# Another order of the first loads, eight zero products and fewer copies of the means at the start of a fused attention and two-layer MoE kernel

## The chip, the cores and the metric

The kernel runs on one core of a Trainium2 chip. The metric is the device time of one launch in microseconds. Three timed runs of the kernel before took 476.56, 477.20 and 478.63 us; the median is 477.2 us. The trace is of one further execution, taken with the hardware profiler.

## The reference

Everything is float32. For 2 batches, 8 heads, 768 positions and head size 64, each query attends to the keys less than 16 positions away and to 24 block summaries (for keys the maximum over 32 positions, for values the mean). The result, 1536 tokens of 512 values, goes through two feed-forward layers.

```python
k_sum = k.reshape(B, H, nb, block, D).max(axis=3)
v_sum = v.reshape(B, H, nb, block, D).mean(axis=3)
scores_l = scale * np.matmul(q, k.transpose(0, 1, 3, 2))          # kept where |i - j| < 16
scores_s = scale * np.einsum('bhsd,bhnd->bhsn', q, k_sum) + np.log(block)
a = softmax(np.concatenate([np.where(mask_l, scores_l, -1e9), scores_s], axis=-1))
x = np.matmul(a, np.concatenate([v, v_sum], axis=2))              # to [1536, 512]
h = x @ w_in                                                      # 512 -> 1024
ln = layernorm(h * softmax(h)) * g_ln
x = ln @ w_out                                                    # 1024 -> 512
h = x @ w_in2; g = elu(h); out = g @ w_out2                       # 512 -> 2048 -> 512
```

## The kernel before

A *unit* is 64 queries of one batch, all 8 heads: 24 units, 12 for each batch. For a unit the kernel makes scores (`attn_s`: a window of 96 keys and the 24 summaries, 120 columns for a pair of heads), the softmax, the transposes of the probabilities (`attn_p`) and, for two units together, the product with v (`attn_x`), whose result `x_ps` is written as a high and a low part (`xT`) for the first feed-forward layer. There (`ffn1_in`) every product is three products of high and low parts (L108 to L110), and so are those behind it. The words of w_in come as 64-bit numbers; each of the 8 blocks of 512 KB goes through a conversion on four engines: L126 on ScalarE, L129 on GpSimd, L130 and L134 on VectorE, then the high part on ScalarE (L138) and the low part on VectorE (L105).

The means of a batch's values (`sum_v`) are products of all its v rows with a small matrix `avg`: six blocks of 256 KB for batch 1 (b = 0), three of 512 KB for batch 2 (b = 1), whose rows VectorE first adds in pairs (L196). The names are the kernel's, which counts batches from 0: the text calls them batch 1 and batch 2. For b = 0 the 24 rows of means go from PSUM to `vsum` (L199, ScalarE), and `attn_x` copies them on GpSimd (L101) into the rows 96 to 119 of the four v buffers `vws`, whose rows 0 to 95 are loaded for each unit (`load_v`).

The order has two sources. On SyncE, which issues all loads, it is the order of the code (a manual schedule): `load_k(0)`, `load_q(1)`, `load_v(0)` and so on in the listing below. On the other engines a scheduler sets it when the program is built, from the order of the code as a priority and its own model of the engines; each engine then works through its list in order. So a moved load or a new instruction can change the lists of all engines. The lists before and after are in the same order again for the last 1753 of some 2340 instructions on TensorE and the last 190 of 213 on SyncE.

At the start, 32 products of zeros (L478) run on TensorE while the first transfers are on their way. Scores, transposes, products with v, means and the other small results share one pool of four PSUM buffers (tag `b`).

Of the kernel before, what the change touches and what calls it, by code (L numbers as in the profile page):

```python
# [24 lines left out]
WIN = 96  # L25
# [13 lines left out]
NV = 4  # L39
# [14 lines left out]
def tile_kernel(ctx: ExitStack, tc: tile.TileContext, qd, kT, v, w_in, w_out, g_ln, w_in2, w_out2,  # L54
# [113 lines left out]
    def load_k(b):  # L168
        k_sb[b] = p_k.tile([128, NP, S + 2 * PAD], F32, tag="k", name="k_sb", bufs=2)
        for p in range(NP):  # L170
            nc.sync.dma_start(k_sb[b][:, p, :], kT[b, p])
# [9 lines left out]
    def sum_v(b):  # L181
        pst = psb.tile([128, DM], F32, tag="b", name="vs_ps")
        v_sb = p_k.tile([128, NP, S + 2 * PAD], F32, tag="k", name="v_sb", bufs=2).rearrange("p a s -> p (a s)")
        m = 2 if b else 1
        n = S // (128 * m)
        if b:
            pairs_d = avg_d.rearrange("(r two) c -> r two c", two=2)[:, 0, :]
            nc.sync.dma_start(avg[0:64, 8:], pairs_d[:, 8:])
            nc.sync.dma_start(avg[64:128, 8:], pairs_d[:, 4:124 + NB])
        for i in range(n):  # L190
            vt = v_sb[:, i * m * DM:(i + 1) * m * DM].rearrange("p (s d) -> p s d", s=m)
            r0 = PAD + i * 128 * m
            nc.sync.dma_start(vt, v[b, r0:r0 + 128 * m, :].rearrange("(p s) d -> p s d", s=m))
            c0 = NB - i * 4 * m
            if b:
                nc.vector.tensor_tensor(vt[:, 0], vt[:, 0], vt[:, 1], op=ALU.add)  # L196
            nc.tensor.matmul(pst, lhsT=avg[:, c0:c0 + 128], rhs=vt[:, 0], start=i == 0, stop=i == n - 1)
        vsum[b] = p_at.tile([128, DM], F32, tag="vsum", name="vsum", bufs=1)
        nc.scalar.activation(vsum[b][WIN:KW, :], pst[WIN:KW, :], AF.Copy)  # L199

    def load_q(n):
        q_bd[n] = p_at.tile([128, NP, 2 * TQ], F32, tag="q", name="q_bd", bufs=4)
        nc.sync.dma_start(q_bd[n], qd[n])
# [13 lines left out]
    def attn_s(n):  # L217
        b, t = divmod(n, NT)
        j, half = divmod(n, 2)
        kw = kws[n % NKW]  # L220
        if n not in q_bd:
            load_q(n)
        if t < NKW and n:
            copy_pool(kw[:, :, WIN:KW], ksum[b])
        if n < NCOPY:
            copy_pool(kw[:, :, 0:WIN], k_sb[b][:, :, t * TQ:t * TQ + WIN])
        sps = psb.tile([128, NP, 128], F32, tag="b", name="s_ps")
        for p in range(NP):
            nc.tensor.matmul(sps[:, p, 0:KW], lhsT=q_bd[n][:, p, :], rhs=kw[:, p, :], start=True, stop=True)  # L229
        sm = p_at.tile([128, NP, KW], F32, tag="sm", name="sm", bufs=NBUF)  # L230
        st = p_at.tile([128, 4, NP], F32, tag="st", name="st", bufs=NBUF)
        nm, ss, ri = (st[:, i, :] for i in range(3))
        mi = 1 if t == 0 else (2 if t == NT - 1 else 0)
        for p in range(NP):
            nc.vector.tensor_tensor_reduce(sm[:, p, :], sps[:, p, 0:KW], mask[:, mi, :], -scale, 3.0e38,  # L235
                                           op0=ALU.add, op1=ALU.min, accum_out=nm[:, p:p + 1])
        for p in range(NP):
            nc.scalar.activation(sm[:, p, :], sm[:, p, :], AF.Exp, bias=nm[:, p:p + 1], scale=-1.0,  # L238
                                 accum_out=ss[:, p:p + 1])
        nc.vector.tensor_scalar(ri, ss, 1e-9, None, op0=ALU.add)  # L240
        nc.vector.reciprocal(ri, ri)  # L241
        for p in range(NP):
            nc.gpsimd.tensor_scalar(sm[:, p, :], sm[:, p, :], ri[:, p:p + 1], 1.0, op0=ALU.mult, op1=ALU.mult)  # L243
        live[n] = sm
    def attn_p(n):
        pps = psb.tile([128, NP, 128], F32, tag="b", name="p_ps")
        for p in range(NP):
            nc.tensor.transpose(pps[:KW, p, :], live[n][:, p, :], ident)  # L248
        pT = p_at.tile([128, NP, 128], F32, tag="pT", name="pT")
        nc.scalar.activation(pT[:KW], pps[:KW], AF.Copy)  # L250
        live[n] = pT

    def attn_x(j):
        xT[j] = [p_at.tile([128, NP, 128], F32R, tag=f"x{i}", name="xT", bufs=3) for i in range(2)]
        xps = psb.tile([128, NP, 128], F32, tag="b", name="x_ps")
        for half in (1, 0):
            n = 2 * j + half
            b, t = divmod(n, NT)
            if b == 0 and t < NV:
                copy_pool(vws[n % NV][WIN:KW, :], vsum[b][WIN:KW, :])  # L260
        todo_x = [(half, p, hh) for half in (1, 0) for p in range(NP) for hh in range(2)]

# [191 lines left out]
    def more(n=1):  # L454
        for _ in range(n):
            if conv:
                conv.pop(0)()
# [16 lines left out]
    zero = ln_t[:, 4, 0:256].bitcast(BF16)  # L474
    nc.vector.memset(ln_t[:, 4, 0:256], 0.0)
    busy = psh.tile([128, F1], F32, tag="h", name="busy")
    for i in range(32):
        nc.tensor.matmul(busy[:, 0:512], lhsT=zero[:, 0:128], rhs=zero, start=True, stop=True)  # L478

    loads = tc.manual_schedule(engines={mybir.EngineType.SP})  # L480
    loads.__enter__()
    load_k(0)
    load_q(1)
    load_v(0)
    nc.sync.dma_start(mask, mask_d)
    sum_k(0)
    nc.sync.dma_start(ident, ident_d)
    load_q(0)
    more()
    nc.sync.dma_start(avg, avg_d)  # L490
    attn_s(0)
    more()
    attn_s(1)
    sum_v(0)
    more(2)
    attn_p(0)
    attn_p(1)
    attn_s(2)
    load_v(1)
    attn_x(0)  # L500
    nc.sync.dma_start(gT, g_ln)
    attn_s(3)
# [301 lines left out]
```

## Time and profile before

| | us |
|---|---|
| median of three runs | 477.2 (476.56 to 478.63) |
| the profiled execution | 476.27 |
| its span in the trace | 474.5 |
| TensorE products busy (PE) | 460.4, 97% of the span |
| weight loads (PEld, beside the products) | 388.4, 82% |
| VectorE (DVE) | 300.1, 63% |
| ScalarE (ACT) | 288.2, 61% |
| GpSimd (POOL) | 116.9, 25% |
| DMA, 82.74 MB | mean 174 GB/s over the span |

A busy share is a mean over the whole span. The stretches differ: the first 37 us move 350 GB/s, those from 100 to 400 us 145 GB/s. In the rows, a time is counted from the span's start; "idle before <- X" is the time for which the engine had nothing running before an instruction and what ended that time; L numbers are lines of the listing. The granted clock of TensorE is 1.00 in all stretches up to 400 us.

### The profile page before, as it was taken

The page shows a single profiled execution, that of the slowest core. Times are in us where ns is not written, and L with a number is a line of the kernel's source. Part 1 is how long each engine was busy: PE and PEld are TensorE (multiplying, and loading weights), DVE is VectorE, ACT ScalarE, POOL GpSimd, SP SyncE. Part 2 cuts the span into 40 slices and gives each one's busy share as a digit, 9 for nine tenths or more (in the row PEclk, how much of TensorE's full clock was granted, in tenths as well). Part 3 has the DMA queues.
Part 4 walks back from the last instruction along what each step waited for, and adds up shares of the span by engine and source line. Part 5 has one row for each costly group of instructions (what it writes and reads, how often), then busy time and mean ns, then how long its engine had stood idle before and what let it go on. Part 6 is the DMA issues. An engine that isn't in the chain of part 4 may idle for free.

```text
span 474.5 us, 7422 instructions
## 1 busy us (share of the span) xinstructions
PE 460.4 (97%) x2597; PEld 388.4 (82%) x2597; DVE 300.1 (63%) x668; ACT 288.2 (61%) x647; POOL 116.9 (25%) x209
## 2 busy tenths in 40 slices
PE   7779999999999999999999999999999999999996
PEld 3556888899989999999888888888888888888884
DVE  3789889875477448986989972476657555460001
ACT  1796899976576537667766762487667665560001
POOL 2786585762444113422132000000000000000000
PEclk9999999999999999999999999999999999999998
DMA  8998987812352424597798324532121221488012
GB/s 272 357 355 296 340 253 228 251 48 84 115 166 83 128 90 133 174 370 255 230 368 329 138 89 135 175 133 90 44 90 44 88 90 45 138 330 259 27 44 89
DMA packets 39989, 82.74 MB, mean 174 GB/s; under 512 B 9648, under 2 KB 18608, under 8 KB 39952
## 3 DMA queue, kind: packets, MB, share of 16 engines
q1 hardware_dynamic: 39808, 82.14, 51.7%
q8 instruction: 20, 0.33, 0.3%
q14 instruction: 17, 0.14, 0.1%
q10 hardware_dynamic: 144, 0.13, 0.1%
HBM read 70.53 MB, written 11.53 MB: 173 GB/s over the span
## 4 chain that ended last, share of the span: by engine, by line
PE 87%; DMA 8%; DVE 2%; ACT 1%; issue 1%; SPq 0%; DVEq 0%; ACTq 0%
PE o_ps L110 9%; PE o_ps L109 9%; PE o_ps L108 9%; PE h L108 7%; PE h L109 7%; PE h L110 7%; PE c L110 5%; PE c L109 5%; PE c L108 5%; DMA y<-in_w_in 5%; PE y_ps L108 4%; PE y_ps L110 4%; PE y_ps L109 4%; PE s_ps L229 3%; PE x_ps L265 2%; PE p_ps L248 2%
## 5 line engine op out<-in xcount | busy, mean ns | idle before, releaser
L129 POOL TENSOR_SCALAR conv<-conv 128x512 f32<-128x512 f32 x48 | 33.8, 705 | 81.2 <-ACT conv L126 79.9
L108 PE MATMUL o_ps<-w4r,g_hl 128*128 128x512 f32 x128 | 49.8, 389 | 0.0
L243 POOL TENSOR_SCALAR sm<-sm,st 128x120 f32<-128x120 f32 x96 | 43.3, 469 | 26.6 <-DVE st L241 7.7
L109 PE MATMUL o_ps<-w4r,g_hl 128*128 128x512 f32 x128 | 49.8, 389 | 0.0
L110 PE MATMUL o_ps<-w4r,g_hl 128*128 128x512 f32 x128 | 45.4, 389 | 0.0
L108 PE MATMUL y_ps<-lnT,w_out 128*128 128x384 f32 x128 | 43.5, 340 | 0.2 <-ACT y L327 0.2
L109 PE MATMUL y_ps<-lnT,w_out 128*128 128x384 f32 x128 | 43.1, 337 | 0.0
L110 PE MATMUL y_ps<-lnT,w_out 128*128 128x384 f32 x128 | 42.8, 336 | 0.0
L108 PE MATMUL h<-w_in,xT 128*128 128x512 f32 x96 | 39.7, 415 | 1.9 <-ACT w_in L138 1.0
L110 PE MATMUL h<-w_in,xT 128*128 128x512 f32 x96 | 38.5, 401 | 0.3 <-DVE xT L105 0.3
L238 ACT ACTIVATE sm<-sm,st 128x120 f32<-128x120 f32 x96 | 36.7, 387 | 3.4 <-DVE st L235 2.5
L109 PE MATMUL h<-w_in,xT 128*128 128x512 f32 x96 | 38.5, 401 | 0.0
L605 ACT ACTIVATE y<-y 128x512 f32<-128x512 f32 x48 | 30.1, 629 | 0.8
L624 DVE COPY y<-o_ps 128x512 f32<-128x512 f32 x5 | 3.5, 691 | 42.9 <-PE o_ps L110 42.9
L235 DVE CUSTOM_DVE_ANT_0 sm<-s_ps,mask 128x120 f32<-128x120 f32 x96 | 21.7, 276 | 12.0 <-PE s_ps L229 11.9
L126 ACT ACTIVATE conv<-y 128x512 f32<-128x512 f32 x30 | 20.1, 675 | 14.2 <-DMA y<-in_w_in 11.7
L105 DVE TENSOR_TENSOR g_hl<-y,g_hl 128x512 fp32r<-128x512 f32 x32 | 22.0, 688 | 10.6 <-ACT g_hl L138 10.6
L229 PEld LDWEIGHTS s_ps<-kw,q_bd 128*128 128x128 f32 x192 | 24.1, 191 | 5.6 <-POOL kw L101 2.4
L130 DVE TENSOR_SCALAR conv<-conv 128x512 int32<-128x512 int32 x48 | 23.7, 493 | 7.5 <-POOL conv L129 7.5
L229 PE MATMUL s_ps<-kw,q_bd 128*128 128x120 f32 x192 | 25.3, 276 | 3.1 <-DMA q_bd<-in_qd 2.8
L109 PEld LDWEIGHTS o_ps<-w4r,g_hl 128*128 128x128 f32 x128 | 24.1, 188 | 5.0
L108 PEld LDWEIGHTS o_ps<-w4r,g_hl 128*128 128x128 f32 x128 | 24.0, 188 | 5.0
(155 smaller groups left out, 1217.2 us busy)
## 6 DMA issues: line engine op xcount, KB each, us to landing
w4r<-w4d SPq DMA_DIRECT2D x38, 512.0 KB, 3.3
y<-in_w_in SPq DMA_DIRECT2D x16, 512.0 KB, 6.2
w4d<-w3f SPq DMA_DIRECT2D x16, 512.0 KB, 3.2
y<-in_w_out SPq DMA_DIRECT2D x14, 512.0 KB, 5.3
q_bd<-in_qd SPq DMA_DIRECT2D x24, 256.0 KB, 5.2
bits<-in_w_out SPq DMA_DIRECT2D x10, 512.0 KB, 5.7
w4l<-w4d SPq DMA_DIRECT2D x10, 512.0 KB, 7.0
vw<-in_v SPq DMA_DIRECT2D x24, 192.0 KB, 5.7
```

Of the source, the lines that this page charges most:

```text
L105: nc.vector.tensor_tensor(out_, x, hi.bitcast(F32), op=ALU.subtract)
L108: nc.tensor.matmul(ps, lhsT=l[0][ls], rhs=r[0][rs], start=first, stop=False, skip_group_check=parts)
L109: nc.tensor.matmul(ps, lhsT=l[0][ls], rhs=r[1][rs], start=False, stop=False, skip_group_check=parts)
L110: nc.tensor.matmul(ps, lhsT=l[1][ls], rhs=r[0][rs], start=False, stop=last, skip_group_check=parts)
L126: first = nc.scalar.activation(x, high.bitcast(F32), AF.Prelu, scale=TO_F32, alpha=SIGN_TO_28)
L129: nc.gpsimd.tensor_scalar(x, x, MOST, LEAST, op0=ALU.min, op1=ALU.max)
L130: nc.vector.tensor_scalar(a, a, 3, None, op0=ALU.logical_shift_left)
L229: nc.tensor.matmul(sps[:, p, 0:KW], lhsT=q_bd[n][:, p, :], rhs=kw[:, p, :], start=True, stop=True)
L235: nc.vector.tensor_tensor_reduce(sm[:, p, :], sps[:, p, 0:KW], mask[:, mi, :], -scale, 3.0e38, op0=ALU.add, op1=ALU.min, accum_out=nm[:, p ...
L238: nc.scalar.activation(sm[:, p, :], sm[:, p, :], AF.Exp, bias=nm[:, p:p + 1], scale=-1.0, accum_out=ss[:, p:p + 1])
L243: nc.gpsimd.tensor_scalar(sm[:, p, :], sm[:, p, :], ri[:, p:p + 1], 1.0, op0=ALU.mult, op1=ALU.mult)
L605: nc.scalar.activation(m, m, AF.Exp, scale=-1.0)
```

## The change

Five edits, all at the start of the program.

- `sum_v(0)` has no `vsum` tile of its own: ScalarE writes the means into `vws[0]`, and VectorE writes them from PSUM into `vws[1]`. `attn_x` copies only for units 2 and 3, from `vws[0]`.
- Unit 0's queries are loaded right behind the keys, then the mask, then unit 1's queries; unit 0's v rows come behind the identity matrix.
- Unit 1's v rows are loaded behind the v rows of the means, ahead of blocks 2 and 3 of w_in ("words 2 and 3").
- Eight more products of zeros are ordered behind unit 1's scores, with high priority.
- `attn_s` returns its last product, so that these can be put behind it.

```diff
-        vsum[b] = p_at.tile([128, DM], F32, tag="vsum", name="vsum", bufs=1)
+        vsum[b] = p_at.tile([128, DM], F32, tag="vsum", name="vsum", bufs=1) if b else vws[0]
         nc.scalar.activation(vsum[b][WIN:KW, :], pst[WIN:KW, :], AF.Copy)
+        if b == 0:
+            nc.vector.tensor_copy(vws[1][WIN:KW, :], pst[WIN:KW, :])
...
-            nc.tensor.matmul(sps[:, p, 0:KW], lhsT=q_bd[n][:, p, :], rhs=kw[:, p, :], start=True, stop=True)
+            last = nc.tensor.matmul(sps[:, p, 0:KW], lhsT=q_bd[n][:, p, :], rhs=kw[:, p, :], start=True, stop=True)
...
+        return last
...
-            if b == 0 and t < NV:
+            if b == 0 and 1 < t < NV:
                 copy_pool(vws[n % NV][WIN:KW, :], vsum[b][WIN:KW, :])
...
-    for i in range(32):
-        nc.tensor.matmul(busy[:, 0:512], lhsT=zero[:, 0:128], rhs=zero, start=True, stop=True)
+    def keep_busy(n, after=None):
+        with tc.issue_after(after.ins) if after else ExitStack():
+            with tc.high_priority():
+                for i in range(n):
+                    nc.tensor.matmul(busy[:, 0:512], lhsT=zero[:, 0:128], rhs=zero, start=True, stop=True)
+
+    keep_busy(32)
...
     load_k(0)
+    load_q(0)
+    nc.sync.dma_start(mask, mask_d)
     load_q(1)
-    load_v(0)
-    nc.sync.dma_start(mask, mask_d)
     sum_k(0)
     nc.sync.dma_start(ident, ident_d)
-    load_q(0)
+    load_v(0)
     more()
     nc.sync.dma_start(avg, avg_d)
     attn_s(0)
     more()
-    attn_s(1)
+    keep_busy(8, attn_s(1))
     sum_v(0)
+    load_v(1)
     more(2)
     attn_p(0)
     attn_p(1)
     attn_s(2)
-    load_v(1)
     attn_x(0)
```

The loads on SyncE's list behind the keys, before (`q_bd` are queries, `vw` the v rows of a unit, `y` the words of w_in in their staging buffers, `v_sb` the v rows of the means):

```order
L203 DMA q_bd<-in_qd 128x512
L207 DMA vw_121<-in_v 96x512
L485 DMA mask<-in_mask 128x360
L487 DMA ident<-in_ident 128x128
L203 DMA q_bd<-in_qd 128x512
L117 DMA y_65<-in_w_in 128x1024
L490 DMA avg<-in_avg 128x152
L117 DMA y_65<-in_w_in 128x1024
L193 DMA v_sb<-in_v 128x512 x6
L117 DMA y_66<-in_w_in 128x1024 x2
L203 DMA q_bd<-in_qd 128x512
L207 DMA vw_122<-in_v 96x512
```

And in the changed kernel, the same stretch:

```order
L205 DMA q_bd<-in_qd 128x512
L494 DMA mask<-in_mask 128x360
L205 DMA q_bd<-in_qd 128x512
L497 DMA ident<-in_ident 128x128
L209 DMA vw_121<-in_v 96x512
L117 DMA y_65<-in_w_in 128x1024
L500 DMA avg<-in_avg 128x152
L117 DMA y_65<-in_w_in 128x1024
L193 DMA v_sb<-in_v 128x512 x6
L209 DMA vw_122<-in_v 96x512
L117 DMA y_66<-in_w_in 128x1024 x2
L205 DMA q_bd<-in_qd 128x512
```

The first queries are now those of unit 0, the second those of unit 1, and `vw_122` (unit 1's v rows) has passed two blocks of words and one of queries. Ahead of the first block of words stand the same five transfers.

VectorE's list around the three adds of batch 2 (`v_sb<-v_sb`), before (L130 and L134 are conversions of words, the first L105 writes the low part of a block of w_in, L240 and L241 belong to the softmax of units 5 and 4):

```order
L240 TENSOR_SCALAR st<-st 128x4
L196 TENSOR_TENSOR v_sb<-v_sb 128x512
L241 RECIPROCAL st<-st 128x4
L105 TENSOR_TENSOR w_in_90<-conv,w_in_89 128x512
L130 TENSOR_SCALAR conv<-conv 128x512
L196 TENSOR_TENSOR v_sb<-v_sb 128x512
L134 SCALAR_TENSOR_TENSOR conv<-y_67,conv 128x512
L240 TENSOR_SCALAR st<-st 128x4
L196 TENSOR_TENSOR v_sb<-v_sb 128x512
L241 RECIPROCAL st<-st 128x4
```

And now (two lines further down in the listing for L240 and L241):

```order
L196 TENSOR_TENSOR v_sb<-v_sb 128x512
L242 TENSOR_SCALAR st<-st 128x4
L130 TENSOR_SCALAR conv<-conv 128x512
L243 RECIPROCAL st<-st 128x4
L134 SCALAR_TENSOR_TENSOR conv<-y_67,conv 128x512
L196 TENSOR_TENSOR v_sb<-v_sb 128x512 x2
L242 TENSOR_SCALAR st<-st 128x4
L130 TENSOR_SCALAR conv<-conv 128x512
```

The low part of the block of w_in stands ahead of the first add now, the other four between the first and the second, and nothing between the second and the third.

TensorE's list around the means of batch 2 (`vs_ps`) up to the products of units 2 and 3 with v (`x_ps`), before:

```order
L248 MATMUL p_ps<-ident,sm 120x128 x3
L108 MATMUL h<-w_in_89,xT 128x512
L197 MATMUL vs_ps<-v_sb,avg 128x512
L109 MATMUL h<-w_in_90,xT 128x512
L110 MATMUL h<-w_in_89,xT 128x512
L197 MATMUL vs_ps<-v_sb,avg 128x512 x2
L108 MATMUL h<-w_in_89,xT 128x512
L229 MATMUL s_ps<-kw_119,q_bd 128x120 x4
L265 MATMUL x_ps<-pT,vw_124 64x64 x8
```

And now:

```order
L252 MATMUL p_ps<-ident,sm 120x128 x3
L109 MATMUL h<-w_in_90,xT 128x512
L110 MATMUL h<-w_in_89,xT 128x512
L197 MATMUL vs_ps<-v_sb,avg 128x512 x2
L108 MATMUL h<-w_in_89,xT 128x512
L197 MATMUL vs_ps<-v_sb,avg 128x512
L231 MATMUL s_ps<-kw_119,q_bd 128x120 x4
L269 MATMUL x_ps<-pT,vw_124 64x64 x8
```

The products of h that stood between the first mean and the second stand ahead of the first, and one stands ahead of the third mean instead of behind it. The eight zero products stand between unit 1's scores and the first mean of batch 1, where nothing stood.

## Rows read from the trace of the kernel before

**Rows 1.** Stretches A:B in us, busy time of each engine, granted clock, DMA share, GB/s.

```profile
2.50:37.00 34.50, 27.01 (x155) 16.47 (x153) 23.81 (x81) 20.28 (x67) 22.93 (x42) 1.00 1.03 350
...
55.00:100.00 45.00, 44.76 (x370) 38.76 (x369) 39.82 (x136) 44.19 (x134) 29.79 (x57) 1.00 0.78 235
```

**Rows 2.** What TensorE waited for, 40 to 460 us: total, times, longest.

```profile
PE s_ps L229 <- DVE xT L105: 0.2, 1, 0.2
PE y_ps L108 <- ACT y L327: 0.2, 1, 0.2
```

**Rows 3.** The chain of waits, 0 to 45 us: start, duration, what.

```profile
26.71 6.91 DMA v_sb<-in_v
...
38.54 1.12 PE vs_ps L197 x2
...
39.90 0.88 PE s_ps L229 x8
40.78 1.08 PE x_ps L265 x32
```

**Rows 4.** TensorE in order of time, 1 to 27 us: start, duration, idle before.

```profile
11.68 2.02 PE L229 MATMUL s_ps<-kw,q_bd 128*128 128x120 f32 x16 [1.90 <-DMA q_bd<-in_qd]
15.16 1.96 PE L197 MATMUL vs_ps<-v_sb,avg 128*128 128x512 f32 x4 [1.47 <-DMA v_sb<-in_v]
...
18.25 2.74 PE L197 MATMUL vs_ps<-v_sb,avg 128*128 128x512 f32 x6
...
22.36 1.12 PE L229 MATMUL s_ps<-kw,q_bd 128*128 128x120 f32 x8 [0.93 <-DMA q_bd<-in_qd]
...
26.82 0.50 PE L108 MATMUL h<-w_in,xT 128*128 128x512 f32 x1 [0.92 <-ACT xT L138]
```

**Rows 5.** ScalarE in order of time, 12 to 28 us.

```profile
12.87 0.69 ACT L126 ACTIVATE conv<-y 128x512 f32<-128x512 f32 x1 [10.87 <-DMA y<-in_w_in]
13.47 0.38 ACT L238 ACTIVATE sm<-sm,st 128x120 f32<-128x120 f32 x1
```

**Rows 6.** TensorE's weight loads in order of time, 0 to 14 us.

```profile
4.13 0.15 PEld L478 LDWEIGHTS <-ln 128*128 128x128 bf16 x1 [0.27 <-issue]
4.44 4.85 PEld L478 LDWEIGHTS <-ln 128*128 128x128 bf16 x23 [0.15 <-issue]
...
11.65 1.86 PEld L229 LDWEIGHTS s_ps<-kw,q_bd 128*128 128x128 f32 x16 [2.36 <-POOL kw L101]
```

**Rows 7.** GpSimd in order of time, 8 to 60 us: the means.

```profile
21.78 3.12 POOL L101 TENSOR_SCALAR vw<-vsum 24x512 f32<-24x512 f32 x4 [0.37 <-ACT vsum L199]
```

**Rows 8.** DMA issues from 27.9 to 28.1 us: count, KB, us to landing.

```profile
v_sb<-in_v SPq DMA_DIRECT2D x1, 512.0 KB, 7.9
```

**Rows 9.** A stretch, columns as in rows 1.

```profile
35.90:37.20 1.30, 1.20 (x5) 0.40 (x3) 1.30 (x4) 0.86 (x3) 1.30 (x2) 1.00 1.04 399
```

**Rows 10.** VectorE in order of time, 34.3 to 38.5 us.

```profile
34.74 0.69 DVE L196 TENSOR_TENSOR v_sb<-v_sb 128x512 f32<-128x512 f32 x1 [0.23 <-issue]
35.35 0.17 DVE L241 RECIPROCAL st<-st 128x4 f32<-128x4 f32 x1
35.44 0.66 DVE L105 TENSOR_TENSOR w_in<-conv,w_in 128x512 fp32r<-128x512 f32 x1
36.02 0.42 DVE L130 TENSOR_SCALAR conv<-conv 128x512 int32<-128x512 int32 x1
36.35 0.77 DVE L196 TENSOR_TENSOR v_sb<-v_sb 128x512 f32<-128x512 f32 x1
37.05 0.68 DVE L134 SCALAR_TENSOR_TENSOR conv<-y,conv 128x512 int32<-128x512 int32 x1
37.65 0.25 DVE L240 TENSOR_SCALAR st<-st 128x4 f32<-128x4 f32 x1
37.80 0.68 DVE L196 TENSOR_TENSOR v_sb<-v_sb 128x512 f32<-128x512 f32 x1
```

**Rows 11.** Groups of instructions, 9 to 100 us: count, busy, mean ns.

```profile
L294 DVE SCALAR_TENSOR_TENSOR ln<-h,ln 128x1024 f32<-128x1024 f32 x6 | 7.2, 1207 | 0.7 <-ACT ln L292 0.7
```

## The prediction

> **What bounds the kernel now.** I read the stretches first, then TensorE's waits. Between 2.5 and 37 us TensorE is busy for 27.0 of 34.5 us, and in the same stretch the DMA engines are busy all the time (share 1.03, 350 GB/s) [rows 1]. From 40 to 460 us TensorE waits only twice, for 0.2 us each [rows 2]. So the kernel has two halves. After 40 us the end is set by the sum of TensorE's work, of which the change moves only the order. Before 40 us the transfers set the pace, and what counts is when TensorE's queue gets past its last wait.
>
> The chain of waits says which that is: the transfer of batch 2's v rows (`v_sb<-in_v`), the third product of the means of batch 2 (38.54 us), the scores of unit 6 (39.90), the products with v of units 2 and 3 (40.78), and from there on TensorE alone [rows 3]. The reader should therefore ask of each edit one thing: does it bring forward the moment at which the products of units 2 and 3 start (40.78 us), and does it move work of TensorE from behind that moment to ahead of it? The second can be counted in the order: ahead of these products stand 16 products of h, 8 transposes and 4 groups of scores behind the first product of unit 1 with v, before as now. So only the first is left.
>
> **The change part by part.**
> Queries. Before, unit 0's queries are the ninth transfer and TensorE idles 1.90 us for them, from the end of the zero products to 11.68 us [rows 4]. Now they take the place of unit 1's, and the scores of unit 0 can start when the zero products end, at 9.8 us: 1.9 us earlier. What is queued behind them eats this. ScalarE's queue still has the first conversion of w_in ahead of all exponentials. That instruction waited 10.87 us for its words and started at 12.87, and the exponentials ran back to back from 13.47 on [rows 5]. The bytes ahead of those words are the same as before (queries, mask, identity, one v block, in another order), so they land at the same time, and the exponentials start at 13.47 again. Gain on the path: 0. If the words came with the scores, the whole 1.9 us would be there; that end I keep for a rival.
>
> Eight zero products behind unit 1's scores. At full rate the 23 loads for zero products of the start are (4.85 - 0.15) / 22 = 0.21 us apart, earlier ones 0.15 + 0.27 = 0.42 us apart [rows 6]. Eight are 1.7 to 3.4 us. They begin at about 11.5 to 12 us, and what follows, the means of batch 1, waits for v rows until 15.16 [rows 4], which have the same bytes ahead of them as before. Even at the slow rate they end at about 15.3. Cost 0; if that cover were gone it would be 1.7 us.
> Do they buy anything? The scores at 11.65, behind the longest idle stretch (1.90 us), load their weights 1.86 / 16 = 0.116 us apart [rows 6]; the scores of unit 6 at 39.90, with TensorE busy around them, take 0.88 us for eight, 0.110 each [rows 3]. Half the rate would show as twice the spacing. So the clock was not lost before. [...] By the row they only replace idle time that has done no harm.
>
> v rows of unit 1 ahead of words 2 and 3. One block of 192 KB moves ahead of 1,024 KB of words and 256 KB of queries; these come 0.5 to 0.7 us later (192 KB at 350 GB/s is 0.56). The scores of unit 2 waited 0.93 us for those queries and started at 22.36 [rows 4]; they stand ahead of the products of units 0 and 1 in TensorE's order and will start at about 23.0. Means to v buffers: the four copies on GpSimd took 3.12 us from 21.78 [rows 7]; now ScalarE writes one buffer directly, VectorE copies the second (0.6 to 0.7 us, by the other passes over 512 columns), and two copies are left. So both halves of x run together behind the scores of unit 2: 23.0 + 1.0 + 1.1 = 25.1 us, and h can start at 25.1 + 0.7 for xT's high half on ScalarE (its other passes over 512 columns take 0.69 [rows 5]) = 25.8 instead of 26.82 [rows 4]. That is 1.0 us, real and early. It isn't kept: the same 16 products of h then stand before the means of batch 2, which wait for v rows, so TensorE idles 1 us longer there.
>
> Those v rows. All bytes ahead of them are the same and the queue is never empty [rows 1], so they land as before. The second of three pieces, issued at 28.0, took 7.9 us and landed at 35.9 [rows 8]; the third is 512 KB more, at 399 GB/s 1.3 us [rows 9]: 37.2. VectorE adds each pair of rows. Before, the third add started at 37.80, with no idle time ahead of it [rows 10], so it came 0.5 us after its data: VectorE's order held it up. In the new order the low half of a converted word (L105) is gone from between the first add and the second, and the third add follows the second at once. By the starts of before [rows 10]: first add 34.74 + 0.61, then 0.15 (L240), 0.33 (L130), 0.09 (L241), 0.60 (L134): second add at 36.5, third at about 37.3, when its rows are there. On TensorE a means' product starts 0.74 us after its add (37.80 to 38.54), so the second at 37.26; its two passes take 0.86 (six take 2.74 with the last one's end [rows 4], 0.43 each), to 38.12; one product of h 0.23; the third means' product 38.35 to 39.21, and then the scores of unit 6. By the same count they started at 38.54 + 0.86 + 0.23 = 39.63 before. Difference 0.4 us. The ends: if VectorE gets to its adds no sooner, 0; if the third product follows the landing with nothing in between, 37.2 + 0.74 + 0.86 = 38.8 for the scores, 0.8 us.
>
> Sum: queries 0, zero products 0, v rows and means 0 (1.0 us gained and lost again), order of the adds -0.4, stalls behind 40 us as before. The profiled execution took 476.27 us for a span of 474.5; it becomes 475.9. The runs shown have their median at 477.2, 0.9 above it, so the forecast as a median is 476.8, with 476.4 to 477.2 as its own range.
>
> **The rivals.**
> The whole gain of the start arrives. If the scores' 1.9 us passed through, or the 1.9 and the 0.9 us at 26.82 together, the median would be 475.3 to 474.4. For it: TensorE's idle time before 37 us is 7.5 us, far more than that. Against it: DMA share 1.03 over the same stretch, and the same bytes ahead of the v rows of batch 2. It would need v rows that land earlier.
>
> Nothing changes. Between the first add and the second now stand an L240 that waits for unit 5's exponentials on ScalarE and an L130 that waits for GpSimd; if one of them is late by 0.4 us, so are the adds, and the gain is gone: 477.2.
>
> Slower, one mechanism: the passes over 1024 columns. Between 55 and 100 us ScalarE is busy for 44.2 of 45 us and VectorE for 39.8 [rows 1], and the one wait there is scores that need the buffer which xT's low half on VectorE gives back (0.2 us) [rows 2]. The instructions of this stretch stand in another order now, and in ScalarE's the exponential of the first h stands ahead of the third xT, where before it came after it. One pass of LayerNorm over 1024 columns on VectorE takes 1.21 us [rows 11]; wherever it now gets ahead of a low half of xT with less than that to spare, TensorE stalls for about 1 us. One such place against the 0.4 us gained gives 477.8, three give 479.8; from the first on the time is above the one before, from the third on by more than can be mistaken. Against it: before, an order of the same kind, with both engines as full, gave one stall of 0.2 us in 45 us.
>
> [...]
>
> **How the numbers follow.** Forecast 0.50 (476.8); whole gain 0.15; nothing 0.18; slower 0.15; clock 0.02. The range for 8 in 10 is 475.0 to 478.6: it leaves out the far part of the whole gain and the slower case from the second stall on. A time that differs by less than 0.5%, 2.4 us, can't be told from no change here. Faster by more than that: 0.06 of the whole gain (its far end, with luck in the stalls) and the clock's 0.02, 0.08. Slower by more than that: the slower case with three such places or more, 0.07. Within: 0.85.
>
> **What would show it right or wrong.** Scores of unit 0 at 9.8 to 10 us and the first exponential still at 13.4 to 13.5: the first step holds; an exponential before 12.9 breaks it. Zero products that end before 15.0 and a first product of the means at 15.0 to 15.3. Scores of unit 2 at 23.0, later than before, and h from about 25.8. A wait of TensorE of 1 us or more for the first add of batch 2, then the third add at 37.2 to 37.4, and products of units 2 and 3 at 40.1 to 40.6. From there to 460 us idle time of TensorE under 1 us in all. I am wrong if the products of units 2 and 3 start before 39.9, since then the transfers did not hold them, or if TensorE stalls by more than 1.5 us behind 40 us.

## The result: slower, 479.8 us against 476.6, and the profile after

The changed kernel has a median of 479.76 us (22 runs, 477.85 to 482.13), the kernel before, run beside it, 476.63 us (22 runs). The ratio is 1.0059, with an interval of 1.0048 to 1.0070: 3.1 us slower, beyond the 0.5% that can be told from no change. The forecast was 476.8. The profiled execution took 480.66 us for a span of 478.9, 0.9 us above its median.

The stretches of the changed kernel, with the columns of [rows 1]:

```profile
2.50:37.00 34.50, 28.91 (x162) 17.09 (x161) 22.13 (x79) 19.11 (x63) 19.91 (x37) 1.00 1.03 351
37.00:40.00 3.00, 1.39 (x3) 0.39 (x3) 3.00 (x6) 1.78 (x6) 2.75 (x4) 1.00 0.74 204
40.00:45.00 5.00, 5.00 (x39) 3.14 (x39) 2.86 (x12) 1.49 (x3) 4.58 (x9) 0.66 0.17 36
```

Up to 37 us the transfers run as before (351 GB/s). Then TensorE is busy for 1.39 of 3 us, and from 40 to 45 us its granted clock is 0.66, where in the profile before it was 1.00 everywhere up to 400 us; from 40.1 to 43.4 us it is 0.50. TensorE in order of time (start, duration, what, idle before):

```profile
10.41 1.94 PE L231 MATMUL s_ps<-kw,q_bd 128*128 128x120 f32 x16
12.19 1.89 PE L486 MATMUL busy<-ln 128*128 128x512 bf16 x8
15.31 1.96 PE L197 MATMUL vs_ps<-v_sb,avg 128*128 128x512 f32 x4 [1.23 <-DMA v_sb<-in_v]
...
23.87 1.12 PE L231 MATMUL s_ps<-kw,q_bd 128*128 128x120 f32 x8 [2.29 <-DMA q_bd<-in_qd]
24.92 1.15 PE L269 MATMUL x_ps<-pT,vw 120*64 120x64 f32 x32
...
27.70 0.50 PE L108 MATMUL h<-w_in,xT 128*128 128x512 f32 x1 [0.55 <-ACT xT L138]
...
36.80 1.13 PE L197 MATMUL vs_ps<-v_sb,avg 128*128 128x512 f32 x2 [0.60 <-DVE v_sb L196]
39.54 1.61 PE L197 MATMUL vs_ps<-v_sb,avg 128*128 128x512 f32 x2 [1.61 <-DVE v_sb L196]
...
41.37 1.91 PE L197 MATMUL vs_ps<-v_sb,avg 128*128 128x512 f32 x2
43.07 1.24 PE L231 MATMUL s_ps<-kw,q_bd 128*128 128x120 f32 x8
44.24 0.98 PE L269 MATMUL x_ps<-pT,vw 120*64 120x64 f32 x26
```

Read it beside [rows 4] and [rows 3]. The start is better: the scores of unit 0 begin 1.3 us earlier, though the means of batch 1 begin 0.15 us later. The loss begins at unit 2's queries: TensorE stands idle for 2.29 us instead of 0.93, h starts at 27.70 instead of 26.82, the second product of the means of batch 2 waits 1.61 us, and from there the same products take longer: two passes of a mean 1.61 and 1.91 us, where before they took 1.12. The scores of unit 6 start 3.3 us later (43.07 against 39.73, or 39.90 as the chain counts), the span ends 4.4 us later; the other 1.1 us are lost behind.

VectorE around the adds, and GpSimd beside them:

```profile
35.91 0.83 DVE L196 TENSOR_TENSOR v_sb<-v_sb 128x512 f32<-128x512 f32 x1 [0.17 <-issue]
36.66 0.57 DVE L242 TENSOR_SCALAR st<-st 128x4 f32<-128x4 f32 x1
37.15 0.41 DVE L130 TENSOR_SCALAR conv<-conv 128x512 int32<-128x512 int32 x1
37.48 0.16 DVE L243 RECIPROCAL st<-st 128x4 f32<-128x4 f32 x1
37.60 0.87 DVE L134 SCALAR_TENSOR_TENSOR conv<-y,conv 128x512 int32<-128x512 int32 x1
38.39 1.69 DVE L196 TENSOR_TENSOR v_sb<-v_sb 128x512 f32<-128x512 f32 x2
```

```profile
36.29 0.93 POOL L129 TENSOR_SCALAR conv<-conv 128x512 f32<-128x512 f32 x1
37.29 0.64 POOL L101 TENSOR_SCALAR kw<-k_sb 128x384 f32<-128x384 f32 x1
38.01 0.93 POOL L129 TENSOR_SCALAR conv<-conv 128x512 f32<-128x512 f32 x1
```

The second add starts 2.48 us after the first; before it was 36.35 - 34.74 = 1.61 [rows 10]. And its product starts at 39.54, so the add ended just ahead of that, 1.1 us after its start and 0.6 us after GpSimd's L129 ended (38.01 + 0.93).

What TensorE waited for in the changed kernel from 45 to 100 us (total, times, longest), where before there was one wait of 0.2 us:

```profile
PE p_ps L252 <- DVE xT L105: 0.3, 1, 0.3
PE h L108 <- ACT xT L138: 0.3, 1, 0.3
```

### The profile page after: what moved, and what is told of

It reads as the page before. It is cut to its first block, busy times and chain, and to the rows that moved or that the text cites. A ratio compares the mean times of both kernels' runs of the same rounds, so it can differ in the third digit from the quotient of the medians.

```text
span 478.9 us, 7434 instructions
## 1 busy us (share of the span) xinstructions
PE 464.9 (97%) x2605; PEld 390.2 (81%) x2605; DVE 301.3 (63%) x669; ACT 287.6 (60%) x647; POOL 118.2 (25%) x207
## 4 chain that ended last, share of the span: by engine, by line
PE 87%; DMA 6%; ACT 3%; DVE 2%; SPq 1%; issue 1%; DVEq 0%
PE o_ps L109 9%; PE o_ps L108 9%; PE o_ps L110 9%; PE h L108 7%; PE h L110 7%; PE h L109 7%; PE c L110 5%; PE c L109 5%; PE c L108 5%; PE y_ps L108 5%; PE y_ps L109 5%; PE y_ps L110 5%; DMA y<-in_w_in 3%; PE s_ps L231 2%; PE x_ps L269 2%; PE t_ps L314 2%
## 5 line engine op out<-in xcount | busy, mean ns | idle before, releaser
L129 POOL TENSOR_SCALAR conv<-conv 128x512 f32<-128x512 f32 x48 | 36.1, 754 | 82.1 <-ACT conv L126 79.1
L240 ACT ACTIVATE sm<-sm,st 128x120 f32<-128x120 f32 x96 | 36.7, 388 | 4.3 <-DVE st L237 4.3
L105 DVE TENSOR_TENSOR g_hl<-y,g_hl 128x512 fp32r<-128x512 f32 x32 | 22.0, 687 | 10.3 <-ACT g_hl L138 10.3
L231 PEld LDWEIGHTS s_ps<-kw,q_bd 128*128 128x128 f32 x192 | 24.5, 193 | 4.6 <-DVE conv L130 2.5
L109 PEld LDWEIGHTS o_ps<-w4r,g_hl 128*128 128x128 f32 x128 | 24.1, 188 | 5.0
L108 PEld LDWEIGHTS o_ps<-w4r,g_hl 128*128 128x128 f32 x128 | 24.0, 188 | 5.0
L110 PEld LDWEIGHTS o_ps<-w4r,g_hl 128*128 128x128 f32 x128 | 24.0, 188 | 5.0
```

The costliest lines, as they stand in the source:

```text
L105: nc.vector.tensor_tensor(out_, x, hi.bitcast(F32), op=ALU.subtract)
L108: nc.tensor.matmul(ps, lhsT=l[0][ls], rhs=r[0][rs], start=first, stop=False, skip_group_check=parts)
L109: nc.tensor.matmul(ps, lhsT=l[0][ls], rhs=r[1][rs], start=False, stop=False, skip_group_check=parts)
L110: nc.tensor.matmul(ps, lhsT=l[1][ls], rhs=r[0][rs], start=False, stop=last, skip_group_check=parts)
L129: nc.gpsimd.tensor_scalar(x, x, MOST, LEAST, op0=ALU.min, op1=ALU.max)
L231: last = nc.tensor.matmul(sps[:, p, 0:KW], lhsT=q_bd[n][:, p, :], rhs=kw[:, p, :], start=True, stop=True)
```

## The experiments

Three theories. **R**: the moved v rows of unit 1 are the loss, by the longer hole ahead of unit 2's scores and the clock that falls behind it. **L** (O in the expectations up to e9): the loss is the new order of the engines' lists, which the scheduler draws anew with every edit to the means or the loads. **Z** (Q in e3): the zero products or the early queries cost. C in e5 is the clock's part of R, and E in e12 to e14 is the edits themselves, whatever the lists. Ratios are to the kernel before, on the same chip.

| run | what it is | ratio | interval |
|---|---|---|---|
| | the change | 1.0059 | 1.0048 to 1.0070 |
| e1 | the change, v rows back | 1.0042 | 1.0025 to 1.0059 |
| e2 | the change without the eight zeros | 1.0052 | 1.0031 to 1.0072 |
| e3 | the change, queries back | 1.0050 | 1.0030 to 1.0069 |
| e4 | the change, zeros between the means | 1.0052 | 1.0034 to 1.0070 |
| e5 | as e4, and zeros ahead of unit 2 | 1.0032 | 1.0018 to 1.0047 |
| e6 | before, with queries and zeros | 1.0011 | 0.9992 to 1.0030 |
| e7 | before, with the direct means | 1.0041 | 1.0024 to 1.0057 |
| e8 | the change, means of batch 2 later | 1.0093 | 1.0070 to 1.0116 |
| e9 | the change without the direct means | 1.0065 | 1.0040 to 1.0091 |
| e10 | as e6, and zeros ahead of unit 2 | 0.9996 | 0.9975 to 1.0016 |
| e11 | as e6, means of batch 2 later | 1.0212 | 1.0183 to 1.0242 |
| e12 | the change in the old lists | 1.0027 | 1.0010 to 1.0044 |
| e13 | v rows back, in the new lists | 1.0037 | 1.0017 to 1.0057 |
| e14 | before, with the v rows moved, old lists | 1.0017 | 0.9997 to 1.0037 |
| e15 | as e12, and zeros ahead of unit 2 | 1.0022 | 1.0007 to 1.0037 |
| e16 | v rows back, in the old lists | 0.9989 | 0.9974 to 1.0005 |

**e2 and e3: not the zeros, not the queries.** Each undoes one edit and leaves all other instructions where they are.

```diff
-    keep_busy(8, attn_s(1))
+    attn_s(1)
```

> The changed kernel without the eight zero products; all other instructions of all engines in the same order. Theories R and O: the products fill idle time only, so the ratio stays 1.005 to 1.007, and the clock falls at 40 us as with them. Theory Z (the products themselves cost, by delaying the means of batch 1 or by what they do to the clock): the ratio goes to 0.999 to 1.002, and the clock stays 1.00 from 40 to 45 us.

> The changed kernel with the order of the first loads as before (unit 1's queries and unit 0's v rows ahead of the mask, unit 0's queries behind the identity matrix); no other instruction moves on any engine. Theories R and O: the scores of unit 0 go back to about 11.7 us and nothing behind 13 us changes, ratio 1.005 to 1.007. Theory Q (the early queries cost through what they delay): ratio 0.999 to 1.003.

Both stay slow, so Z falls. But the clock did differ: in e2's profile, without the zeros, TensorE ran the first means behind 3.09 us of idle time at a granted clock of 0.50 (14.3 to 17.6 us), four passes in 3.46 us instead of 1.96, and at 38 us it ran at 0.50 again (38.2 to 41.5 us):

```profile
14.62 3.46 PE L197 MATMUL vs_ps<-v_sb,avg 128*128 128x512 f32 x4 [3.09 <-DMA v_sb<-in_v]
...
38.11 2.07 PE L197 MATMUL vs_ps<-v_sb,avg 128*128 128x512 f32 x2 [1.51 <-DVE v_sb L196]
```

The first of these cost nothing: unit 2's scores still waited for their queries (0.16 us, at 22.55).

**e1, e7 and e9: rows without means, means without rows.**

The edit below is e1's, against the change.

```diff
     sum_v(0)
-    load_v(1)
     more(2)
...
     attn_s(2)
+    load_v(1)
     attn_x(0)
```

> The changed kernel, with unit 1's v rows loaded again where they were before (behind unit 2's queries); the order of the queries, the zero products and the direct means stay. Theory R (the moved rows): they push the words, unit 2's queries and with them the products of units 0 and 1 back, TensorE stands idle before the means of batch 2 and its clock falls. Then without the move the scores of unit 2 start at about 22.4 us, the granted clock stays 1.00 from 40 to 45 us, and the ratio to the kernel before is 0.998 to 1.001. Theory O (the new order of VectorE's and TensorE's lists, which comes with the direct means): the loss stays, ratio 1.004 to 1.007.

> The kernel before with one edit alone: the means straight to two v buffers. No load moves, but the lists of all engines come out in another order (the same as with the v rows back, but without the new order of queries and without the zero products). Theory O: the new order costs behind 45 us, where with the v rows back TensorE waited 1.3 us for low parts of xT: ratio 1.003 to 1.005. Theory R (the moved rows): 0.998 to 1.001.

> The changed kernel without the direct means: new order of queries, eight zero products, v rows of unit 1 ahead of the words. With the runs so far it completes a square: neither the moved rows nor the direct means 1.0011, direct means without the moved rows 1.0042, both 1.0059. Theory O (the direct means alone cost, by the order of the lists that they bring): 0.999 to 1.002. Theory R (the moved rows cost too, by the later queries of unit 2 and the longer hole, about 1 us): 1.002 to 1.004.

All three are slower, 1.0041 to 1.0065, so neither edit alone is the loss. e1 lost its 0.0042 with the granted clock at 1.00 from 40 to 45 us, and e9 lost more than either theory had said. In e7 no load moved at all: its scores of unit 6 start 0.7 us later than before (40.44 us), and it loses twice that behind 45 us. TensorE's waits there, and its busy time from 45 to 100 us (columns as in [rows 1]), in e7 and, in the third fence, in the kernel before; last, VectorE ahead of e7's longest wait:

```profile
PE p_ps L250 <- DVE xT L105: 1.3, 2, 1.0
PE h L110 <- DVE xT L105: 0.5, 1, 0.5
```

```profile
45.00:100.00 55.00, 53.27 (x444) 45.77 (x443) 48.74 (x170) 49.89 (x156) 35.55 (x72) 1.00 0.88 262
```

```profile
45.00:100.00 55.00, 54.76 (x452) 47.20 (x451) 48.70 (x173) 51.92 (x160) 34.47 (x71) 1.00 0.82 257
```

```profile
75.47 1.21 DVE L292 TENSOR_REDUCE st<-h 128x1 f32<-128x1024 f32 x1
76.61 0.67 DVE L134 SCALAR_TENSOR_TENSOR conv<-y,conv 128x512 int32<-128x512 int32 x1
...
77.29 0.65 DVE L105 TENSOR_TENSOR xT<-x_ps,xT 128x512 fp32r<-128x512 f32 x1
```

1.5 us of TensorE are gone, in waits for low parts of xT on VectorE. A pass over 1024 columns stands ahead of the low part at 77.29 us, with a conversion of words between them: the mechanism of the rival that the prediction called slower. But the edits to the means, and e9's to the loads, had brought lists of their own, so these runs can't part lists from edits.

**e4 and e5: the clock.** e4 adds eight zero products to the sum of the means of batch 2, e5 eight more ahead of unit 2's scores.

```diff
+            if b and i == 0:
+                for _ in range(8):
+                    nc.tensor.matmul(pst, lhsT=zero[:, 0:128], rhs=zero, start=False, stop=False)
```

> The changed kernel with eight more zero products (1.7 us at full rate), added to the means of batch 2 between their first and their second product, where TensorE now stands idle for 1.6 to 2.2 us. Theory R with the clock: the granted clock stays 1.00 from 40 to 45 us, the scores of unit 6 start at 41.4 to 41.8 us instead of 43.07, and of the 3.1 us lost 1.5 to 1.7 come back: ratio 1.002 to 1.003. If the clock is only a companion of the loss: ratio 1.006 as before, or 1.007 to 1.009 where the products delay the second mean.

> The changed kernel with eight more zero products in each of two holes of TensorE: ahead of unit 2's scores (where it stood idle for 2.3 us) and between the first and the second mean of batch 2. Theory C (the two longer holes let the granted clock fall for a stretch, in most executions, at one place or another before 45 us, which costs 1.6 to 1.9 us): no stretch before 45 us has a granted clock under 1.00, and the ratio to the kernel before is 1.001 to 1.003. With zeros in one hole alone the ratio was 1.0052, which theory C puts down to the other hole. Theory O (the order of the lists alone, no clock): 1.005 to 1.006 again.

The scheduler drew other lists for these two, the same for both but not the change's, so only e4 against e5 tells of the hole alone. e4's profiled execution had a granted clock of 1.00 in all stretches from 2.5 to 474 us, had the scores of unit 6 at 40.12 and took 477.0 us, but its median is 479.3, and five of its ten runs had a mean granted clock of 0.994 to 0.996, as the changed kernel's. With both holes filled all 12 runs had a mean granted clock of 0.997 or more, and the ratio is 1.0032; it differs from e4's by no more than the two intervals allow. Of the 22 runs of the changed kernel, 16 had 0.992 to 0.996 (median 480.0 us) and 6 had 0.998 to 1.000 (478.2). This mean also counts the end of the program, where TensorE stands idle in part (0.90 from 460 to 475 us in the kernel before), so it is no proof by itself; what it is worth is worked out below, and e13 has the price.

**e6: what is free.**

> The kernel before with two of the edits alone: the order of the first loads and the eight zero products. All other instructions keep the lists of the kernel before. All theories that put the loss on the moved v rows or on the new lists: ratio 0.998 to 1.001, scores of unit 0 at 9.5 to 10 us, adds and means of batch 2 as in the kernel before. If the early queries or the products cost anything: 1.002 or more.

1.0011, with 1.000 inside its interval: as expected. The diff is the change's own, for those two edits.

**e8 and e11: the means of batch 2 out of the way.** Two misses.

```diff
-        if t == 0:
+        if t == 1:
             sum_v(1)
```

> The changed kernel with the means of batch 2 (loads, adds, products) and the load of batch 2's keys taken two steps of the first layer later, behind the products of units 2 and 3 instead of ahead of them. If the loss comes from the path over the adds of batch 2 and the hole ahead of them, it is gone: products of units 2 and 3 at 36 to 39 us, no half clock at 38 to 44 us, ratio 0.995 to 1.000. If the loss comes from the stretch behind 45 us (passes over 1024 columns in another order), the ratio stays above 1.002.

> The kernel before with the new order of queries and the eight zero products, and with the means of batch 2 one step of the first layer later, so that two loads of queries go ahead of their v rows and the products of units 2 and 3 stand ahead of the means in TensorE's list. If the wait for these v rows is what the first 40 us are worth, the products of units 2 and 3 start at 36 to 38 us instead of 40.6 and the ratio is 0.993 to 0.998. If the words and the softmax hold these products just as long, or the hole only moves behind them, 0.999 to 1.003.

The edit above is e11's; e8 has t == 2, and loads the keys of batch 2 one step later. The products of units 2 and 3 did come at 37.93 and 36.93 us, but nothing stood ready behind them. In e11:

```profile
40.48 0.50 PE L108 MATMUL h<-w_in,xT 128*128 128x512 f32 x1 [1.73 <-ACT xT L138]
43.24 0.50 PE L110 MATMUL h<-w_in,xT 128*128 128x512 f32 x1 [1.75 <-DVE xT L105]
50.41 2.74 PE L197 MATMUL vs_ps<-v_sb,avg 128*128 128x512 f32 x6
```

The loads behind, the keys of batch 2 first, wait for these means (2.5 us for their products in the kernel before, 4.0 in the change): in e11 the DMA engines were all but idle from 40 to 50 us (share 0.03), and the loss was 10 us. So the means at 36 to 40 us are not only a gate; what follows needs them there.

**e10: zeros in the old lists.**

> The kernel before with the new order of queries and the eight zero products, and with six more zero products ahead of unit 2's scores; all other instructions stay in the lists of the kernel before. If the kernel before also loses its clock in some executions in the hole ahead of unit 2's scores, the runs above 477 us become rarer: ratio 0.997 to 0.999. If it does not, 1.000 to 1.001.

0.9996 with an interval of 0.9975 to 1.0016: no gain that can be told. Its runs with a mean granted clock of 0.996 or less were 3 of 12, against 8 of 16 of the kernel before beside it.

**e12, e13, e14, e16: one without the other.** The lists are held by a chain over the instructions of TensorE, VectorE, ScalarE and GpSimd; LISTS is a table of numbers, the order of one kernel or the other. Nothing else is new.

```diff
+    for name, runs in LISTS.items():
+        mine = [i for i in nc.cur_bb.bb.instructions if i.engine == getattr(mybir.EngineType, name)]
...
+        for one, two in zip(wanted, wanted[1:]):
+            tc.add_manual_dep(two, one.name, mybir.DependencyInfo(
+                mybir.DependencyClass.NoSync, mybir.DependencyReason.DATA), reason="lists")
```

> The whole change, but with all instructions of TensorE, VectorE, ScalarE and GpSimd held in the order that they have in the kernel before (the eight zero products, VectorE's copy of the means and the two copies that are left stand where they must). Theory L (the lists are the loss): adds and means of batch 2 as in the kernel before, no wait of TensorE over 0.5 us from 45 to 100 us, ratio 0.997 to 1.002. Theory E (the edits themselves cost, through the moved rows and the clock): 1.004 to 1.006.

> The changed kernel with unit 1's v rows loaded again behind unit 2's queries, and with all instructions of the other engines held in the order of the changed kernel: one transfer moves and nothing else. Theory L: 1.004 to 1.006, as the changed kernel. Theory E: 0.999 to 1.002. If both have a part, 1.003 to 1.004, the rows' part being the hole ahead of unit 2's scores and the clock that falls in it.

> The kernel before with unit 1's v rows loaded ahead of words 2 and 3, and all instructions of the other engines held in its own order: one transfer moves and nothing else. The scores of unit 2 come 0.6 us later. Theory L: 0.998 to 1.002. Theory E: 1.002 to 1.005.

> The changed kernel with unit 1's v rows loaded again behind unit 2's queries and with all instructions of the other engines held in the order of the kernel before; what stays of the change is the order of the first queries, the eight zero products and the means written straight to two buffers. If moved rows and new lists are the whole loss, the ratio is 0.998 to 1.001 (1.0011 without the direct means). If the direct means cost something of their own, it is 1.002 to 1.003, as with the whole change in the old lists (1.0027).

With the queries, zeros and direct means of the change in all four, the square is

| | old lists | new lists |
|---|---|---|
| v rows in their old place | 0.9989 (e16) | 1.0037 (e13) |
| v rows moved | 1.0027 (e12) | 1.0059 (the change) |

Both theories have a part. The new lists cost 0.0032 to 0.0048, 1.5 to 2.3 us; the moved rows 0.0022 to 0.0038, 1.0 to 1.8 us. The intervals are 0.001 to 0.002 to either side, so whether the two add up exactly stays open, and the smaller figure for the rows, 0.0022 in the new lists, is no larger than its own uncertainty. e16 also ran beside a slower sample of the kernel before (477.47 us, against 476.36 beside e12 and e13); by the times alone both parts measured against it are 1.7 us. Without both, the change costs nothing, and gains nothing that can be told.

The lists' part, in e13 (its line numbers are 8 higher; VectorE, GpSimd, then TensorE):

```profile
35.16 0.69 DVE L204 TENSOR_TENSOR v_sb<-v_sb 128x512 f32<-128x512 f32 x1 [1.19 <-issue]
35.77 0.48 DVE L250 TENSOR_SCALAR st<-st 128x4 f32<-128x4 f32 x1
36.15 0.42 DVE L138 TENSOR_SCALAR conv<-conv 128x512 int32<-128x512 int32 x1
36.49 0.17 DVE L251 RECIPROCAL st<-st 128x4 f32<-128x4 f32 x1
36.60 0.98 DVE L142 SCALAR_TENSOR_TENSOR conv<-y,conv 128x512 int32<-128x512 int32 x1
37.50 1.37 DVE L204 TENSOR_TENSOR v_sb<-v_sb 128x512 f32<-128x512 f32 x2
```

```profile
35.21 1.01 POOL L109 TENSOR_SCALAR kw<-k_sb 128x384 f32<-128x384 f32 x1
36.30 0.73 POOL L137 TENSOR_SCALAR conv<-conv 128x512 f32<-128x512 f32 x1
```

```profile
22.18 1.12 PE L239 MATMUL s_ps<-kw,q_bd 128*128 128x120 f32 x8 [0.93 <-DMA q_bd<-in_qd]
...
38.23 1.13 PE L205 MATMUL vs_ps<-v_sb,avg 128*128 128x512 f32 x2 [1.20 <-DVE v_sb L204]
39.43 1.02 PE L205 MATMUL vs_ps<-v_sb,avg 128*128 128x512 f32 x2
40.28 1.05 PE L239 MATMUL s_ps<-kw,q_bd 128*128 128x120 f32 x8
41.26 1.15 PE L277 MATMUL x_ps<-pT,vw 120*64 120x64 f32 x32
```

The hole ahead of unit 2's scores is 0.93 us again, yet the second add starts 2.34 us after the first, and TensorE waits 1.20 us for it. In all profiles in the old lists (before, e6, e10, e12, e14, e15, e16) the second add starts 1.60 to 1.61 us after the first, and TensorE is busy for 54.76 us from 45 to 100 us; in e13 for 54.10, in the change for 54.40. Against e16, which has the same loads in the old lists, e13's scores of unit 6 start 0.4 us later and TensorE is busy for 0.7 us less from 45 to 100 us; the spans differ by 1.3 us (475.9 and 474.6).

The clock's price is here too, since e13 and the change have the same lists: from the second mean of batch 2 to the products of units 2 and 3 it is 41.26 - 38.23 = 3.03 us, and in the change, at a granted clock of 0.50 from 40.1 to 43.4 us, 44.24 - 39.54 = 4.70. That is 1.7 us for one such stretch.

The rows' part, in e12 (first fence) and e16 (second):

```profile
23.00 1.12 PE L239 MATMUL s_ps<-kw,q_bd 128*128 128x120 f32 x8 [1.77 <-DMA q_bd<-in_qd]
...
40.63 1.05 PE L239 MATMUL s_ps<-kw,q_bd 128*128 128x120 f32 x8
```

```profile
22.77 1.12 PE L239 MATMUL s_ps<-kw,q_bd 128*128 128x120 f32 x8 [1.13 <-DMA q_bd<-in_qd]
...
39.84 1.05 PE L239 MATMUL s_ps<-kw,q_bd 128*128 128x120 f32 x8
```

In these two executions the rows cost 0.8 us, at a granted clock of 1.00 from 2.5 to 45 us in both. In e14, where one transfer moved and nothing else, the hole was 2.43 us, up to 24.48, and the granted clock stayed at 1.00 up to 37 us; then came this stretch at 0.50:

```profile
37.50:40.80 3.30, 3.30 (x6) 1.67 (x5) 3.30 (x9) 1.74 (x6) 3.30 (x4) 0.50 0.71 207
```

Over all profiles: of ten executions with the rows moved six had such a stretch before 45 us, at 14, 24, 30, 37, 38 or 40 us, and the first add of batch 2 began at 35.9 us in the mean (34.6 to 37.0, nine of them; e8 moves it). Of seven with the rows in place and the means where they were none had one, and the first add began at 35.0 us (34.6 to 35.6).

But seven profiles are few, and the timed runs say otherwise of the kernel before. In the 18 profiles the mean granted clock is 0.988 to 0.996 where TensorE had a stretch of lower granted clock near the start (0.50 over 3.3 us in six of them, in e11 0.83 from 40 to 50 us), and 0.997 to 1.000 where it did not. By this sign 59 of the 122 timed runs of the kernel before beside e1 to e16 had such a stretch too (median 477.4 us; the other 63 476.2): its profile is one of those without. The runs of the square by the same sign, first how many had a stretch, then the median of the others:

| | old lists | new lists |
|---|---|---|
| v rows in their old place | 7 of 12, 476.3 us (e16) | 4 of 12, 478.3 us (e13) |
| v rows moved | 7 of 12, 477.1 us (e12) | 16 of 22, 478.2 us (the change) |

With the clock kept, the new lists cost 1.2 to 2.0 us, so most of their part is not the clock. The moved rows cost 0.7 us in the old lists, as in the two executions above, without more stretches; in the new lists they cost nothing with the clock kept, and go with more stretches. The groups are small and were sorted after the fact, so this is a reading and not a test.

**e15: does filling the hole bring it back?**

> As e12 (the whole change in the old lists), with six more zero products ahead of unit 2's scores. If the hole there lets the clock fall in some executions, the slow ones among them go, and the ratio is 0.001 to 0.003 below e12's; if not, the two agree within 0.001.

1.0022 against 1.0027 can't be told apart. Its profile has a granted clock of 0.50 from 30.5 to 33.8 us instead, beginning less than two us behind the next hole (1.89 us ahead of the first h, at 28.72), and 9 of its 12 runs have the sign of a stretch. How much of the rows' part is the clock and how much the later first add is not settled by a run that changes one of them alone.

## Why the prediction was wrong

*Queries, zero products.* Right. The scores of unit 0 started at 10.41 (9.8 was said), the exponentials still at 13.60 behind the first conversion, and the means of batch 1 at 15.31:

```profile
13.03 0.68 ACT L126 ACTIVATE conv<-y 128x512 f32<-128x512 f32 x1 [11.03 <-DMA y<-in_w_in]
13.60 0.40 ACT L240 ACTIVATE sm<-sm,st 128x120 f32<-128x120 f32 x1
```

e2, e3 and e6 confirm a cost of 0.

*v rows of unit 1.* This is the first step that failed: a term of 0 that measured 1.0 to 1.8 us. The words and queries would "come 0.5 to 0.7 us later", by a sum over bytes. The scores of unit 2 came at 23.87, 1.5 us later, but one execution is not enough to say so: with the rows moved they start at 22.4 to 24.5 (ten profiles, mean 23.5), with the rows in place at 21.9 to 24.4 (eight, mean 22.8), so the sum was right in the mean. What was wrong is what it led to. "1.0 us gained and lost again" had h at 25.8; it started at 27.70. Where the rows stayed and the means were written directly, in e13, h did start at 25.95, and the first add no earlier for it (35.16 against 34.74): there the gain was lost again as said. And that the v rows of batch 2 land as before, since the same bytes are ahead of them, looked at the queue alone. The v rows are added by VectorE, whose list holds the masks of units 4 and 5 ahead of the adds, and these wait for scores that wait for h: what is late at 23 us is late at 35. In the change the masks of unit 5 began at 34.84 us, behind 0.85 us of waiting for their scores, and the first add came behind them.

*Order of the adds.* This step failed too. Sized at -0.4 us, it is +0.7 for the second add (2.34 us behind the first in e13, 1.61 before; the prediction's sum gives 1.78). I took the spacings of [rows 10] for instructions that would stand in another place. From L242 to the next start it is 0.49 us in the change and 0.38 in e13 instead of 0.15, from L134 to the second add 0.79 and 0.90 instead of 0.60. The rival "nothing changes" had named L242 (L240 before) and priced it at 0.4 us, but as a wait for unit 5's exponentials. It is unit 4's: in the change unit 5's last exponential starts at 37.67, after L242 has ended (36.66 + 0.57), and unit 4's had ended by 35.6.
The long passes ended just behind GpSimd's. In the change L242 ends at 37.23 and a GpSimd pass at 37.22 (36.29 + 0.93); in e13 it is 36.25 and 36.22. The second add of the change ends 0.54 us behind GpSimd's L129 (38.01 + 0.93), and L142 of e13 (36.60 + 0.98) 0.55 us behind L137. It is so throughout the 18 profiles: of the adds of v rows and the conversions L134 on VectorE, 67 took more than 0.8 us (the median of all 450 is 0.69), and each of them ended 0.53 to 0.54 us behind the end of a GpSimd instruction; 94 instructions such as L242 (128x4, median 0.17) took more than 0.3 us, and each ended 0.02 to 0.03 us behind one. No run took GpSimd's pass away, so why the one ends behind the other is not shown.

*Stalls behind 40 us as before.* Failed by its size: put at 0, it is 0.4 us of TensorE's time from 45 to 100 us in the change, 0.7 in e13 and 1.5 in e7. The rival "slower" had the right mechanism for e7; it was given a chance of 0.15 because the order before had given one stall. That its time for three stalls, 479.8 us, is the time measured is luck: the change itself has two waits of 0.3 us there. One order with few stalls doesn't say that others have few: of the six new sets of lists here, none reached the 54.76 us of the old one, which came back in every kernel that had it.

*The clock.* "The clock was not lost before" holds for the execution that it was read from (granted clock 1.00 up to 400 us); about half of the timed runs of the kernel before look as if it was. A change of the clock was weighed only as a gain, at 0.02; that it could be lost now was not. No run shows the gain that the 0.02 stood for: in the profile before, TensorE's products between 15.16 and 21.4 us ran at a granted clock of 1.00. The spacing in [rows 6] showed that 1.9 us of idle time had not cost the clock at one place; I took that for all places and never asked what a wider hole would do. What the changed kernel's trace shows is a loss: a granted clock of 0.66 from 40 to 45 us, behind 1.61 us of idle time.

## What to carry to other kernels

Where a scheduler writes the lists, an edit is two changes: itself and a new draw of all lists; hold the lists and time each apart before either is believed. A transfer put ahead of others is priced by the first engine that waits for what it displaced, and followed from there through every list to the end, not by bytes in the queue alone. Where a busy engine has holes, ask what each may cost in clock before one is widened (here 1.7 us for one stretch at 0.50), and don't take one profile with a granted clock of 1.00 for a kernel that keeps it: compare the mean granted clocks of many runs.

## What the runs showed of the hardware

The clock did not fall at one place: in executions of nearly the same program it fell to 0.50 (over 3.3 us each time) at 14, 24, 30, 37, 38 or 40 us or not at all, and the timed runs of one and the same kernel, the one before, had mean granted clocks of 0.992 to 1.000. One such stretch cost 1.7 us where TensorE's work was on the path, and nothing where a transfer was (e2 at 14 us). The place did not go by the length of the idle time ahead alone: the clock fell within 2 us of the end of 1.51 to 3.09 us of idle time (e2, e3, e9, e15 and the change), in e14 behind 1.01 and 0.52 us, and it stayed at 1.00 behind 2.01 us in e8, 1.77 and 1.97 in e12, 2.29 in the change and 2.43 in e14.

The time of a transfer scatters. Of the three loads of the v rows of batch 2, of 512 KB each, the traces have the landing of one, the second: 7.9 us after its issue in the kernel before, 8.6 in the change, and 7.1 to 8.8 over the experiments that did not move the means, with no order by kernel. A forecast to 0.4 us from one execution, as [rows 8] and [rows 9] were used, is finer than that.

VectorE's long passes ended just behind GpSimd's. An addition or conversion over 128x512 with a median of 0.69 us ended, whenever it took over 0.8 us, 0.53 to 0.54 us behind a GpSimd instruction (67 of 67 in 18 profiles).
